# Denominators and Q masks by DMA, the quotient on GpSimd, V products in pairs, zero products as fillers, in a two-branch attention kernel

## The chip, the cores and the metric

The kernel runs on one core of a Trainium2 chip. A core has a matrix engine (PE, TensorE), a vector engine (DVE), a scalar engine (ACT) that computes exponentials, GpSimd (POOL), a sync engine (SP) that here only issues DMAs, and 16 DMA engines. Each engine works through its own instructions in order, and they wait for one another with semaphores. Matrix products are written to PSUM, which has 8 banks of 128 partitions by 512 fp32 numbers; everything else lies in SBUF.

The metric is the device time of one execution in microseconds (us), as the median of several.

## The reference

One input `x` of 2048 positions by 512 features goes through two attention blocks, each with 32 heads of 16 features. A sigmoid gate mixes the two results.

```python
g = sigmoid((x * gate_w).sum(-1, keepdims=True))
# A: linear attention, phi(q) = [softmax(q w), softmax(-q w)], the same for k
kv  = einsum("bhsf,bhsd->bhfd", phi_k, v)
num = einsum("bhqf,bhfd->bhqd", phi_q, kv)
den = einsum("bhqf,bhf->bhq", phi_q, phi_k.sum(s)) + 1e-6
a = (num / den) @ A_wo
# B: ordinary attention
p = softmax((q @ k.T) * 16 ** -0.5)
b = (p @ v) @ B_wo
return g * a + (1 - g) * b
```

B is the large part: 32 heads times 2048 queries times 2048 keys make 134 million exponentials.

## The kernel before

**Tiles.** B is cut into 32 blocks. A block has four heads and 512 queries (`b // 8` is the chunk of queries, `b % 8` the group of heads). For each head there are 16 key tiles of 128 keys, so a block has 64 score tiles of 128 keys by 512 queries, and the kernel has 2048. A score tile is one product with K = 32 rows (`qk_mm`): the four heads of a group use four row strips of the array and can run side by side. Q is kept in `qz` twice, once for the even and once for the odd heads, with the other 16 rows of every 32 at zero.

**Two ways to an exponential.** Most tiles go to ACT (`add_exp`, L776). The tiles of ACT are taken in *slots* of three and two by turns; each slot has its own PSUM banks (`psS` 0 to 2 and 3 to 4), one ACTIVATE makes the exponentials of a slot, and the scores of slot j + 2 can be written only when slot j is read. The rest, `DN[b]` tiles of block b (416 in all), is done by DVE in *groups* of four (`add_group`, L736): a tile is drained to int16 with an added constant (D1, L749, one for each tile, out of the PSUM banks `psM` or `psS` 5), then over a whole group come D2 (L759) and D3 (L761), which split it by bit masks, and D4 (L764, a product). For every third group from the eighth on, GpSimd does D4 in four quarters (L767). Each such tile then needs two products with V (its *terms*, s and t) instead of one. A group may hold tiles of two blocks.

**V products.** `add_pv` multiplies the exponentials of a slot with V (L792). V carries a column of ones, so that row 16 of every 32 output rows is the sum of the weights. The four heads use four column strips of the array and add into one bank, `psO`. The exponentials lie in a ring of ten slots. `add_pvd` adds the terms of DVE's tiles.

**End of a block** (`add_norm`, L861). DVE transposes `psO` to SBUF (T1, L864), which frees the bank for the next block. It then takes the reciprocal of the sums (L867), multiplies (L870, into `TB`), and after each second block transposes back (T2, L874) into `oT`, the left operand of the output products. Those (`out_tile`, L899) add A and B into one bank; DVE scales the sum (L903) and SP writes it out (L887).

**Q.** `q_fill` (L594) makes two groups of heads for 512 queries: four PE products, and two DVE operations (L601) that multiply by the masks for even and odd heads into `qz`.

**Branch A and the rest** fill in beside B: weights and projections (L534, L561), `phi` (L953: two ACT exponentials, L965 and L967 on DVE, a product on GpSimd, L969), `kv_half`, `q_rest`, and the gate (L922, 64 products of one column).

**The order** of every engine's instructions is written out in advance by a planner (`Plan.layout`, L130). It simulates the five engines with a cost for each operation. Of the operations that are ready it takes the one with the lowest priority number. A `dq` (the score product of a DVE tile) or a `term` can ride with a running product of the same kind if its strip is free. PE's busy share in the last 3.4 us of the plan steers the fillers: below `ACTIVE[0]` an idle PE gets a product into a free bank of `psM` or `psS` 5 (L1101), and below `ACTIVE[1]` or `ACTIVE[3]` a score product gets one or two fillers ahead of it, written to its own bank of `psS` (L704). `emit` (L284) then gives each engine its list with the waits. So a wait on the chip holds up all that stands behind it on that engine, also where the plan saw none.

Of the kernel before, what the change touches and what calls it, by code (L numbers as in the profile page):

```python
# [8 lines left out]
BF16 = mybir.dt.bfloat16  # L9
# [20 lines left out]
DN = (0, 8, 10, 13, 11, 9, 13, 11, 3, 11, 7, 11, 13, 15, 18, 6, 15, 14, 18, 10, 15, 17, 20, 12, 17, 15, 16, 20, 16, 18, 17, 17)  # L30
G_EARLY = 8
D_FIRST = 12
RIDE = 0.02
WINDOW = 3.4
ACTIVE = (0.64, 0.66, 0.60, 0.54)
PE_CLASS = {"qk": 0, "dq": 0, "pv": 1, "term": 1}
T_PRIO = -10.0
G_DEEP = 5
K_AT, K_PACE, Q_AT, Q_PACE = 70.0, 8.0, 199.0, 12.5
POOL_GROUPS = tuple(range(8, 110, 3))  # L40
D_AHEAD = 20.0
# [8 lines left out]
class Op:  # L50
    __slots__ = ("eng", "dur", "prio", "fn", "deps", "succ", "nd", "ready", "end", "lat", "sem", "count",
                 "name", "full", "extra", "room", "fill", "bank_of", "acq", "rel", "seq", "clock", "take", "pos", "margin", "done", "kind", "heads", "lock", "tight")

    def __init__(self, eng, dur, prio, fn, name):
        self.eng, self.dur, self.prio, self.fn, self.name = eng, dur, prio, fn, name
        self.deps, self.succ = [], []
        self.lat, self.sem = 0.0, None
# [5 lines left out]
        self.done = False  # L63
        self.kind, self.heads, self.lock = None, (), False
# [20 lines left out]
class Plan:  # L85
# [44 lines left out]
    def layout(self):  # L130
# [16 lines left out]
        last_pe, used_heads, last_cls = None, set(), None  # L147
        lock_end = {"dve": 0.0, "pool": 0.0}
        while left:
# [5 lines left out]
            while finish and finish[0][0] <= t + 1e-9:  # L155
                _, _, phase, op = heapq.heappop(finish)
                op.done = op.done or phase == 1
                for s in op.succ:
# [4 lines left out]
                    else:  # L163
# [3 lines left out]
                        if op.sem is not None:  # L167
                            gap += MARGIN
                    s.ready = max(s.ready, (op.end if phase else op.end - op.lat) + gap)
# [8 lines left out]
            for e in ENGINES:  # L178
# [6 lines left out]
                ride = None  # L185
                if e == "pe" and last_pe is not None and busy[e] > t - 1e-6:
                    want = {"qk": "dq", "pv": "term"}[last_pe]
                    for item in sorted(queues[e]):
                        o = item[2]
                        if o.kind == want and not used_heads & set(o.heads):  # L190
                            if o.acq is not None:
                                bs = [b for b in o.acq.banks if b.free and b.shared]
# [31 lines left out]
                if e == "pe":  # L224
                    while streams and streams[0][1] < t - WINDOW:
                        streams.popleft()
                    active = sum(y - max(x, t - WINDOW) for x, y in streams) / WINDOW
# [21 lines left out]
                if e == "pe" and ride is None:  # L249
                    last_pe, used_heads = (op.kind, set(op.heads)) if op.kind in ("qk", "pv") else (None, set())  # L250
                if e == "pe":
                    if op.room and t > 20.0 and active < ACTIVE[1]:
                        op.extra = min(op.room, 1 if active > ACTIVE[2] else 2)
                        op.full += 0.21 * op.extra
                        op.dur += 0.105 + 0.215 * op.extra
# [4 lines left out]
                    if ride is None:  # L260
                        streams.append((t + op.dur - op.full, t + op.dur))
# [874 lines left out]
```

The softmax here doesn't subtract the row's maximum and nothing guards it: scores larger than these inputs give would overflow.

## Time and profile before

| | us |
|---|---|
| median of 8 runs | 806.74 |
| lowest and highest run | 802.97, 808.21 |
| the profiled execution | 806.11 |
| its span, from the first to the last instruction | 804.2 |
| ACT busy in it | 777.6 |
| PE, DVE, POOL busy in it | 754.3, 692.4, 231.6 |

The groups of instructions that the change touches, from the list of groups by shape (count, busy us and mean ns of one):

| line | engine, operation | count | busy us | mean ns |
|---|---|---|---|---|
| L779 | ACT exponentials, three tiles | 326 | 508.7 | 1560 |
| L779 | ACT exponentials, two tiles | 327 | 372.2 | 1139 |
| L704 | PE fillers ahead of scores | 133 | 47.6 | 406 |
| L1101 | PE fillers in idle time (`psS`, `psM`) | 15, 13 | 5.4, 5.1 | 383, 417 |
| L864 | DVE T1, transpose of `psO` | 32 | 22.5 | 702 |
| L867 | DVE reciprocal, 128x16 | 32 | 7.6 | 237 |
| L870 | DVE multiply into `TB` | 32 | 14.7 | 459 |
| L874 | DVE T2 | 16 | 11.2 | 703 |
| L601 | DVE Q masks (from `psM`, from `psS`) | 18, 12 | 13.0, 8.8 | 723, 736 |

The mean of one instruction is longer than its share of the busy time where instructions of one engine overlap: the 653 exponentials of B together keep ACT busy for 749.8 us, 1.148 us each. Idle time of an engine is put down to the instruction that came after it, and to the one that released that.

### The profile page before, as it was taken

Reading aid. Unit: us, or ns where it says so; the run is one execution under the profiler, and the core shown is the slowest. Engines: PE = TensorE matmul, PEld = TensorE weight load, DVE = VectorE, ACT = ScalarE, POOL = GpSimd, SP = SyncE. Lnnn points to the kernel's source line nnn. Section 1 sums busy time; section 2 is a strip of 40 time slices with the busy share of each in tenths; the row PEclk is TensorE's granted clock in tenths of the full one; section 3 lists DMA queues with packets and bytes.
Section 4 is the critical chain, followed back from the end, with each engine's and each line's share of the span. In section 5 each row is a group of like instructions: output and inputs, shape, how many; then the busy total and the mean of one; then the engine's idle time right before and its main releaser. Section 6 shows DMA issues by size and latency. Waiting matters only on the chain.

```text
span 804.2 us, 14104 instructions
## 1 busy us (share of the span) xinstructions
PE 754.3 (94%) x5959; PEld 229.6 (29%) x5959; DVE 692.4 (86%) x1120; ACT 777.6 (97%) x724; POOL 231.6 (29%) x188
## 2 busy tenths in 40 slices
PE   8999999999999999999899989999989999998899
PEld 4333332333323232232232222322222222212223
DVE  3488878978766898898999999999999999989995
ACT  5999999999999999999999999999999999988996
POOL 5000022252443132522323333242222422342222
PEclk9899999999999999999999999999999999978999
DMA  5600000000100000000000000000000000000000
GB/s 126 138 2 1 1 2 1 1 1 1 54 0 2 1 7 14 1 9 1 1 1 2 2 1 1 1 14 2 15 1 1 7 1 14 8 0 1 1 1 27
DMA packets 18958, 9.30 MB, mean 12 GB/s; under 512 B 13264, under 2 KB 18896, under 8 KB 18896
## 3 DMA queue, kind: packets, MB, share of 16 engines
q1 hardware_dynamic: 17408, 7.74, 3.9%
q8 instruction: 46, 0.75, 0.4%
q10 hardware_dynamic: 1104, 0.66, 0.3%
q0 software_dynamic: 384, 0.02, 0.1%
q14 instruction: 16, 0.13, 0.1%
HBM read 3.69 MB, written 2.10 MB: 7 GB/s over the span
## 4 chain that ended last, share of the span: by engine, by line
ACT 70%; PE 21%; DVE 6%; SPq 1%; issue 1%; POOL 1%; DMA 0%
ACT E_t L779 67%; PE psS L687 6%; PE psO L792 6%; PE psS L534 3%; ACT EA_t L960 3%; PE psM L534 3%; PE psS L704 1%; SPq L431 1%; DVE Tx_t L749 1%; DVE vA_t L749 1%; DVE WB_t L759 1%; POOL WAT_t L767 1%; DVE vA_t L761 1%; PE psM L687 1%; DMA xT_t<-in_A_x_dram 0%
## 5 line engine op out<-in xcount | busy, mean ns | idle before, releaser
L779 ACT ACTIVATE E_t<-psS 128x1536 bf16<-128x1536 f32 (+1 forms) x653 | 749.8, 1349 | 13.0 <-PE psS L687 10.4
L687 PE MATMUL psS<-qz_t,kTB_t 32*128 32x512 bf16 x1831 | 277.9, 390 | 33.3 <-ACT E_t L779 26.6
L792 PE MATMUL psO<-E_t,vaug_t 128*32 128x512 bf16 (+1 forms) x1632 | 242.5, 395 | 0.0
L687 PEld LDWEIGHTS psS<-qz_t,kTB_t 32*128 32x128 bf16 x1831 | 68.2, 91 | 269.5 <-ACT E_t L779 200.7
L767 POOL TENSOR_TENSOR Tx_t<-Tx_t,WB_t 128x512 bf16<-128x512 bf16 x44 | 53.7, 1249 | 144.3 <-DVE WAT_t L761 43.9
L792 PEld LDWEIGHTS psO<-E_t,vaug_t 128*32 128x32 bf16 (+1 forms) x1632 | 56.5, 93 | 128.8 <-issue 124.9
L749 DVE TENSOR_SCALAR Tx_t<-psM 128x512 int16<-128x512 f32 x103 | 70.4, 684 | 22.4 <-PE psM L687 20.5
L767 POOL TENSOR_TENSOR vA_t<-vA_t,WB_t 128x512 bf16<-128x512 bf16 x44 | 53.2, 1239 | 122.7 <-DVE WB_t L759 51.2
L687 PE MATMUL psM<-qz_t,kTB_t 32*128 32x512 bf16 x217 | 84.7, 390 | 2.3 <-DVE Tx_t L749 0.6
L792 PE MATMUL psO<-vA_t,vaug_t 128*32 128x512 bf16 (+1 forms) x304 | 76.2, 389 | 0.0
L749 DVE TENSOR_SCALAR Tx_t<-psS 128x512 int16<-128x512 f32 x85 | 57.8, 681 | 7.1 <-PE psS L687 4.3
L749 DVE TENSOR_SCALAR vA_t<-psS 128x512 int16<-128x512 f32 x71 | 48.3, 680 | 6.5 <-PE psS L687 4.5
L704 PE MATMUL psS<-xT_t,ident_t 128*128 128x512 bf16 x133 | 47.6, 406 | 6.6 <-ACT E_t L779 6.0
L965 DVE TENSOR_REDUCE stat_t<-EA_t 128x64 f32<-128x1024 bf16 x32 | 38.8, 1213 | 16.6 <-ACT EA_t L960 16.3
L969 POOL TENSOR_TENSOR phiK_t<-EA_t,stat_t 128x1024 bf16<-128x1024 bf16 x16 | 33.2, 2079 | 65.0 <-DVE stat_t L967 65.0
L767 POOL TENSOR_TENSOR phiQ_t<-phiQ_t,WoA_t 128x512 bf16<-128x512 bf16 x16 | 18.0, 1154 | 116.5 <-DVE phiQT_t L761 116.5
L792 PE MATMUL psO<-Tx_t,vaug_t 128*32 128x512 bf16 (+1 forms) x188 | 51.4, 383 | 0.0
L767 POOL TENSOR_TENSOR WAT_t<-WAT_t,WB_t 128x512 bf16<-128x512 bf16 x24 | 29.8, 1271 | 64.0 <-DVE WB_t L759 21.5
L749 DVE TENSOR_SCALAR vA_t<-psM 128x512 int16<-128x512 f32 x65 | 44.4, 683 | 4.1 <-PE psM L687 2.9
L969 POOL TENSOR_TENSOR phiQ_t<-EA_t,stat_t 128x1024 bf16<-128x1024 bf16 x16 | 32.3, 2020 | 43.2 <-DVE stat_t L967 43.2
L792 PE MATMUL psO<-WAT_t,vaug_t 128*32 128x512 bf16 (+1 forms) x156 | 44.0, 401 | 0.0
L764 DVE TENSOR_TENSOR Tx_t<-Tx_t,WB_t 128x2048 bf16<-128x2048 bf16 x24 | 29.1, 1211 | 0.1
(177 smaller groups left out, 948.8 us busy)
## 6 DMA issues: line engine op xcount, KB each, us to landing
out_dram<-WvA_t SPq DMA_DIRECT2D x14, 128.0 KB, 1.7
WB_t<-in_B_wqkv_dram SPq DMA_DIRECT2D x3, 384.0 KB, 4.6
WvA_t<-in_A_wqkv_dram SPq DMA_DIRECT2D x1, 512.0 KB, 4.1
WoA_t<-in_A_wo_dram SPq DMA_DIRECT2D x1, 512.0 KB, 3.9
WoB_t<-in_B_wo_dram SPq DMA_DIRECT2D x1, 512.0 KB, 4.9
phiK_t<-in_A_x_dram SPq DMA_DIRECT2D x2, 128.0 KB, 2.8
phiK_t<-in_A_x_dram ACTq DMA_DIRECT2D x2, 128.0 KB, 3.0
WB_t<-in_B_wqkv_dram SPq DMA_DIRECT2D x2, 128.0 KB, 3.8
```

The costliest lines, as they stand in the source:

```text
L431: dma("sp", 0.01 * (4 * c + t), lambda e, c=c, t=t: e.dma_start_transpose(xT[:, t, NQ * c:NQ * (c + 1)], A_x[0, NQ * c:NQ * (c + 1), 128 * ...
L534: return [lambda e, ap, i=i: e.matmul(ap, lhsT=lhs[i], rhs=rhs[i], start=(i == 0), stop=(i == len(lhs) - 1)) for i in range(len(lhs))]
L687: return e.matmul(bank, lhsT=kT_B[32 * i:32 * i + 32, hg // 2, 128 * kt:128 * (kt + 1)], rhs=qz[32 * i:32 * i + 32, (b // 8) % 2, hg, :], ...
L704: e.matmul(psS[:, 512 * base:512 * (base + 1)], lhsT=ident[:], rhs=xT[:, 0, 0:NQ], start=True, stop=True)
L749: ops.append(drain(f, mm, "dve", 0.70, d_prio(d), lambda e, ap, q=q: e.tensor_scalar(quarter(t, q).bitcast(I16), ap, EXPB, 0.0, op0=ALU.ad ...
L764: add(1.24, lambda e: e.tensor_tensor(shaped(t, m), shaped(t, m), m, ALU.mult), [g["m"]], tk, "D4")
L767: ops.append(P.add("pool", 1.0, d_prio(g["ts"][0]) - 5.0, lambda e, q=q: e.tensor_tensor(quarter(t, q), quarter(t, q), quarter(m, q), ALU. ...
L779: op = P.add("act", 0.051 + 0.4267 * n, 0.0, lambda e: e.activation(Ebuf[:, j // 2 % EPAIRS, 1536 * (j % 2):1536 * (j % 2) + 512 * n], psS ...
L792: return e.matmul(psO[32 * i:32 * i + w, :], lhsT=vaug[:, kt, VW * h:VW * h + w], rhs=rhs, start=start, stop=stop, tile_position=(0, 32 * ...
L960: ins = e.activation(EA[:, b, :].rearrange("p (g s c) -> p s g c", s=2, c=64)[:, sgn, :, :], ap.rearrange("p (g c) -> p g c", c=64), ACTF. ...
L965: P.add("dve", 1.22, prio, lambda e: e.tensor_reduce(stat[:, b, 1, :], e3, AX.X, ALU.add), reads=[("EA", b)], writes=[("ss", b)], name=f"s ...
L969: P.add("pool", 2.0, prio, lambda e: e.tensor_tensor(dst.rearrange("p (g f) -> p g f", f=DH), e3, stat[:, b, 1, :].unsqueeze(2).to_broadca ...
```

## The change

- **Q masks.** `q_fill` keeps one DVE operation, a scaled copy of all rows for the even heads. Four DMAs on SP (`qo`) then copy the odd heads' rows to the other half of `qz`, and four more (`qe`) copy zeros over them in the first half. The zeros come from two memsets of `qz` on GpSimd in the beginning, planned at 3.3 and 4.3 us.
- **Weight sums and quotient.** For blocks 0 to 29, DVE copies `psO` as it is to `Tf` (L864's place). The sums go through DRAM: one DMA writes the four rows of sums (`ld`), one reads them back spread over 128 partitions by 16 (`lq`). After each second block four DMAs put the odd heads' rows beside the even ones (`mg`), DVE takes one reciprocal of 128x32, one DMA writes it to DRAM (`lr`), eight read it back, each to 16 partitions (`rb`), and GpSimd multiplies `Tf` by it into `oT`. All these DMAs are on SP. For odd groups of heads the V slice starts 16 columns earlier, so that the result lies in the upper 16 rows. Blocks 30 and 31 keep the old way.
- **Groups end with their block.** All `DN` are even (420 tiles in all), so a block's last group has two or four tiles. `PN` gives the number of groups of each block whose D4 is on GpSimd (33 in all). The buffers go by three phases (blocks 0 to 7, 8 to 13, 14 on) instead of two.
- **V products in pairs.** `hold` makes the V product of an even slot wait for the exponentials of the odd slot after it.
- **Fillers.** Those ahead of score products are gone. A V product with a head that has started gets up to two products of a zero weight tile of 32 columns, added into that head's strip of `psO`. The planner weighs PE's activity by the kind of product (`ROWS` for one to four score tiles side by side, 0.9 and 1.1 for terms and V products), with thresholds of 0.42 to 0.48, and counts riding products in part.
- **Planner and pace.** `dq` and `term` can ride behind one another as well, if they were ready when the stream began. Terms have priority 40 instead of -10. The gate is in four parts. Branch A's K side begins at slot 96 with pace 5 (before: 70 and 8), its Q side at 202 with pace 19 (199 and 12.5), and both are held back by the exponentials of given slots (Q side: slot 260 and every 20 from there).

```diff
-WINDOW = 3.4
-ACTIVE = (0.64, 0.66, 0.60, 0.54)
+WINDOW = 3.41
+ROWS = (0.0, 0.28, 0.58, 0.75, 0.8)
+ACTIVE = (0.46, 0.44, 0.48, 0.42)
-T_PRIO = -10.0
+T_PRIO = 40.0
+PV_SETS, PV_FROM = 2, 0
+DMA_PAD, T2_PAD = 1.0, 1.5
...
+    pool(3.3, -7, lambda e: e.memset(qz[:, 0, 2:8, :], 0.0), writes=["qza"], name="qz0")
+    pool(4.3, -7, lambda e: e.memset(qz[:, 1, :, :], 0.0), reads=["qza"], writes=["qz0"], name="qz1")
...
+    def moves(kind, fn, n, reads, writes, name, lat=2.0):
...
+        op = P.add("sp", 0.07 * n, -40, fn, reads=reads, writes=writes, name=name, sem=chain[kind][0], lat=lat)
+        op.semval = chain[kind][1]
+        op.pad = DMA_PAD
+        return op
...
     def q_fill(r, qc, prio, banks=None, after=()):
...
-        for par in range(2):
...
+        drain(f, mm, "dve", 0.69, prio, lambda e, ap: e.tensor_single_scalar(qz[:, c, 2 * r, :], ap, QSCALE, ALU.mult),
+              writes=[("q", c, 2 * r)], name=f"Qe{r}.{qc}")
+        moves(f"qo{c}{r}", lambda e: [e.dma_start(qz[o, c, 2 * r + 1, :], qz[o, c, 2 * r, :]) for o in z(1)], 4,
+              [("q", c, 2 * r), "qz0"], [("q", c, 2 * r + 1)], f"qo{r}.{qc}")
+        moves(f"qe{c}{r}", lambda e: [e.dma_start(qz[o, c, 2 * r, :], qz[y, c, 2 * r + 1, :])
+                                      for o, y in zip(z(1), z(0))], 4,
+              [("q", c, 2 * r + 1)], [("q", c, 2 * r)], f"qe{r}.{qc}")
...
-            for _ in range(op.extra):
-                e.matmul(psS[:, 512 * base:512 * (base + 1)], lhsT=ident[:], rhs=xT[:, 0, 0:NQ], start=True, stop=True)
...
+    def hold(j):
+        k = j + (PV_SETS - 1 - (j + PV_FROM) % PV_SETS)
+        return [exp_ops[k]] if k > j and k < NS and exp_ops[k] is not None else []
...
+                for _ in range(zero_ops[j, b].extra):
+                    e.matmul(psO[32 * old[0]:32 * old[0] + 32, :], lhsT=zero[:], rhs=xT[:, 0, 0:NQ], start=False, stop=False,
+                             tile_position=(0, 32 * old[0]), skip_group_check=True)
...
     def add_norm(b, pv):
...
+        if b < NB - 2:
+            P.add("dve", 0.69, -50, lambda e: e.tensor_copy(Tf[:, par, :], psO[:]), reads=["psO"], writes=[("Tf", par)],
+                  after=[pv], name=f"ev.{b}")
+            moves(f"ld{par}", lambda e: e.dma_start(ld[par], Tf[16 - par::32, par, :]), 1, [("Tf", par)], [("ld", par)],
+                  f"ld{b}")
+            moves(f"lq{par}", lambda e: e.dma_start(Lq[:, par, :], ld[par].rearrange("i (a c) -> (i a) c", c=16)), 1,
+                  [("ld", par)], [("Lq", par)], f"lq{b}")
+            if par == 1:
+                moves("mg", lambda e: [e.dma_start(Tf[32 * i + 16:32 * i + 32, 0, :], Tf[32 * i + 16:32 * i + 32, 1, :])
+                                       for i in range(4)], 4, [("Tf", 1)], [("Tf", 0)], f"mg{b}")
+                P.add("dve", 0.35, -40, lambda e: e.reciprocal(rd[:], Lq[:]), reads=[("Lq", 0), ("Lq", 1)],
+                      writes=["rd2"], name=f"rd{b}")
+                moves("lr", lambda e: e.dma_start(lr.rearrange("t i (a c) -> (i a) t c", c=16), rd[:]), 1, ["rd2"],
+                      ["lr"], f"lr{b}")
+                moves("rb", lambda e: [e.dma_start(Rb[32 * i + 16 * t:32 * i + 16 * t + 16, :],
+                                                   lr[t, i].unsqueeze(0).to_broadcast([16, D]))
+                                       for i in range(4) for t in range(2)], 8, ["lr"], ["Rb"], f"rb{b}")
+                P.add("pool", 1.1, -40, lambda e: e.tensor_tensor(oT[:, qc % 2, r, :], Tf[:, 0, :], Rb[:], ALU.mult),
+                      reads=[("Tf", 0), "Rb"], writes=[("oT", qc % 2, r)], name=f"T2.{b}").lock = True
+                P.ops[-1].pad = T2_PAD
```

## The prediction

> **What bounds the kernel now.** First the page's busy shares and its slices, then ACT in order of time, then busy time by stage.
>
> ```profile
> PE 754.3 (94%) x5959; PEld 229.6 (29%) x5959; DVE 692.4 (86%) x1120; ACT 777.6 (97%) x724; POOL 231.6 (29%) x188
> ...
> ACT  5999999999999999999999999999999999988996
> ...
> PEclk9899999999999999999999999999999999978999
> ```
>
> ACT works without a break from 20 us to the end, but for the slices where the granted clock of PE dips. ACT's idle time is 804.2 - 777.6 = 26.6 us; 13.0 of it lie before exponentials of B, and 2.7 of these in the first 24 us (2.06, 0.50, 0.16). The rest of B's waits, in ACT's timeline, are 15 gaps of 9.3 us together. The larger ones:
>
> ```profile
> 37.42 1.02 ACT L779 ACTIVATE E_t<-psS 128x1024 bf16<-128x1024 f32 x1 [0.88 <-PE psS L687]
> ...
> 390.70 36.27 ACT L779 ACTIVATE E_t<-psS 128x1024 bf16<-128x1024 f32 x32 [1.37 <-PE psS L687]
> ...
> 605.38 100.75 ACT L779 ACTIVATE E_t<-psS 128x1024 bf16<-128x1024 f32 x89 [0.81 <-PE psM L687]
> ...
> 716.90 18.45 ACT L779 ACTIVATE E_t<-psS 128x1536 bf16<-128x1536 f32 x16 [1.03 <-PE psS L687]
> ```
>
> Now the stretches around these times (columns: us, then busy us and instructions of PE, PEld, DVE, ACT, POOL, then the granted clock):
>
> ```profile
> 383.10:386.50 3.40, 2.30 (x15) 0.67 (x13) 3.27 (x7) 3.40 (x5) 2.14 (x2) 1.00 0.00 0
> 386.50:389.90 3.40, 3.40 (x24) 0.96 (x22) 2.99 (x5) 2.83 (x4) 0.59 (x1) 0.50 0.00 0
> 598.10:601.50 3.40, 2.36 (x14) 0.59 (x12) 3.40 (x7) 3.40 (x4) 0.00 (x0) 1.00 0.00 0
> 601.50:605.00 3.50, 3.50 (x26) 0.55 (x23) 3.09 (x5) 3.00 (x3) 0.00 (x0) 0.51 0.00 0
> 703.90:707.40 3.50, 2.23 (x13) 0.57 (x10) 3.36 (x6) 2.96 (x3) 3.50 (x4) 0.99 0.00 0
> 707.40:717.60 10.20, 10.20 (x40) 1.59 (x39) 7.98 (x13) 7.40 (x7) 0.59 (x1) 0.50 0.00 0
> ...
> 660.00:700.00 40.00, 37.71 (x297) 10.28 (x293) 39.51 (x58) 40.00 (x36) 10.96 (x8) 1.00 0.03 11
> ```
>
> The clock is halved in five stretches: 31.5 to 38.3, 386.5 to 389.9, 601.5 to 605.0, 707.4 to 717.6 and 734.7 to 741.5, 30.7 us in all. Of the 9.3 us of late gaps 8.6 lie in or right behind them, 0.28 us of stall for each us at half clock; the others are 0.54 and 0.17. Just ahead of each halving PE did little: 13 to 15 products in 3.4 us, where the 40 us from 660 have 297, or 25 in 3.4. So the end is set by ACT's work, plus what PE's clock costs it, plus start and tail.
>
> Why PE was thin is seen in the timeline from 702 us on:
>
> ```profile
> 702.69 5.31 POOL L767 TENSOR_TENSOR vA_t<-vA_t,WB_t 128x512 bf16<-128x512 bf16 x4 [10.09 <-DVE WB_t L759]
> ...
> 703.13 1.64 DVE L761 TENSOR_SCALAR vA_t<-Tx_t 128x2048 int16<-128x2048 int16 x1
> ...
> 705.42 0.39 PE L687 MATMUL psS<-qz_t,kTB_t 32*128 32x512 bf16 x1 [1.06 <-DVE Tx_t L749]
> ```
>
> PE waits 1.06 us for DVE to drain a bank, and DVE is late since one mask took 1.64 us beside GpSimd instead of the usual 0.68. At 598 and 731 PE waits for ACT at the end of a block, with V products scarce.
>
> **ACT's work.** 2048 - 420 = 1628 tiles make 651 slots instead of 653, two of two tiles fewer. With 749.8 us for 326 + 327 exponentials and 1560 - 1139 = 421 ns between the forms, one of two tiles costs (749.8 - 326 x 0.421) / 653 = 0.94 us: **-1.9 us**, certain.
>
> **The clock.** From the records I summed PE's stream time (0.213 us for 512 columns, products on different strips once) over the windows of 3.41 us in which the clock changes, with the new planner's weights (0.28, 0.58, 0.75, 0.8 for one to four score tiles side by side, 1.1 for V products and full ones). Of 226 windows at full clock, the end aside, the five just ahead of a halving are the five lowest: 0.22, 0.28, 0.32, 0.32, 0.35; the next is 0.38. So these weights order the windows as the gate does, and it lies at about 0.37. The new thresholds, 0.42 to 0.48, are above it, where the old ones (0.64 and so on) were met in the plan and missed on the chip: both filler banks are the ones DVE was late to free, and the fillers at L704 stand ahead of scores that ACT awaits. A zero product needs no bank, since it adds into `psO`, and delays no score ahead of it. Bounds: all 9.3 us go, or none and more (third rival). I take a third of the 8.6 left over, since the planner's times still differ from the chip's, most around a block's first V product, where no filler may start: **-6.5 us** with the 0.54 and 0.17 partly gone.
>
> What the Trainium skill would have here speaks against a gain ("TensorE: Matmul & The Clock Gate", section "Why this matters for your kernels"): it asks for no PE-idle gap above some 3 us, and no such gap precedes any of the five halvings, so by it the fillers would be worth nothing and the time 804.8. The rows above decide otherwise: products were spaced 1 us apart and the clock fell all the same.
>
> **DVE.** Off: 15 masks x 0.73 = 11.0; 30 reciprocals x 0.237 = 7.1; 30 multiplies x 0.459 = 13.8; 15 T2 x 0.703 = 10.5. On: 15 reciprocals of 128x32, between the rows for 16 and 64 columns (0.237, 0.542), 0.35 taken, 5.1; four tiles' D1, 2.7; 12 half groups instead of five whole ones, about 3 (half-size rows are not shown; bounds 0.34 and 0.69 for D2 and D3); gate 0.5. T1 becomes a copy of the same size (drains of 128x512 take 0.68, T1 0.70). Sum -31 us of 692. DVE is not on the path but in the late stretches (39.5 of 40 us busy from 660), and there it gains little: Q tiles of A, 4.6 us of DVE each by their rows, are now paced up to slot 560 and more, where before the last ran at 528 us, and `PN` gives GpSimd 6 groups of the last eight blocks instead of 11. So I count **0** from it, -0.7 to +2 as bounds.
>
> **GpSimd.** 15 quotients at the 1.15 to 1.27 us of L767 add 18 us, a group more 5, and the memsets, 7168 columns at L486's 0.545 us for 512, 7.6. The memsets stand ahead of `gw` and `Wbd`, which end at 12.2 us and so at 20; their readers come at 40 slots or later. **0.** Queued behind a quotient that waits for `rb` are D4 quarters and `phi` products, and behind these terms on PE. POOL is idle 71% of the time; without that cover a wait of w us delays terms by w.
>
> The Trainium skill states that GpSimd and DVE share a port pair which one of them holds for a whole instruction ("SBUF — State Buffer", section "SBUF: two separate sides"). The 1.64 us mask above agrees. By the rule each of the 15 quotients may hold DVE for its length, 15 x 1.2 = 18 us of DVE; by the row, 15 x (1.64 - 0.68) = 14 us; in both the planner's locks and DVE's free 14% cover it.
>
> **SP.** 15 x 8 for masks, 30 x 2, and 15 x (4 + 1 + 8) are 375 DMAs. An issue takes 0.33 us (output) to 0.45 (x), so SP is busy 124 to 169 us, and the plan's 0.07 is too low. What waits in this queue holds up the others: `qe` for `qo`, `lq` for `ld`, `rb` for `lr`, and outputs behind all. Landing takes 1.7 (output) to 3.0 us (x), planned 2.0 with pads of 1.0 and 0.6, which absorb the issue but for `rb` (8 x 0.38 = 3.0 against 0.56). Q is filled seven blocks ahead. **0**, as long as the quotient's chain fits: `Tf` is free for the next even block only after the quotient. Low end: copy 0.70, three landings of 1.7, reciprocal 0.24, `rb` 7 x 0.33 + 1.7, quotient 1.15: 11 us. High end: 0.71, three of 3.0, 0.54, DVE's queue 1.2, `rb` 7 x 0.45 + 3.0, `mg` 1.8, a Q move 8 x 0.45 + 3.0, a D4 quartet 5.3, 1.27: 33 us. I take 17 (landings of 2.2, issues of 0.38, half a quartet). An even block has at least 48 ACT tiles x 0.459 = 22 us.
>
> **Pairs.** A V product starts one exponential later, up to 1.4 us, and so may a block's copy. The ring of ten slots (11.5 us) covers it; the last slot, 650, is flushed alone, so the tail stays. A change between scores and V products on PE is saved every second slot, worth nothing while PE waits for ACT 200.7 us. **0**, -0.5 to +2.
>
> **Sum.** 804.2 - 1.9 - 6.5 = 795.8 us of span. The profiled execution has 1.9 us outside its span and lies 0.6 below the median: **798.3 us**. Its own range is 795.5 (9.3 + 1.9 off the median) to 801.
>
> **Rivals.**
> 1. *DVE stays the late engine.* For it: 39.5 of 40 us, and PE's 1.06 us wait. A filler cannot pass a blocked PE. Then the three halvings from 600 us on stay and only those at 31 and 386 (1.5 + 1.4 us) go: 806.74 - 1.9 - 2.9 = 802.
> 2. *The quotient's chain outlasts a block.* From 22 us on, the copy of `psO` waits for `Tf`, PE stops at the next block's first V product, the scores behind it are late and ACT stalls. For it: 375 issues on one queue, the in-order waits, the high end of 33. Against it: 17 by the nearest rows. At 4 us in 6 of 15 pairs: +24, 822.
> 3. *The zero products don't hold the clock.* No row shows one. Some 25 windows lie between 0.38 and 0.50; if their fillers fail, each costs 3.4 x 0.28 = 0.95 us: 806.74 - 1.9 + 24 = 829.
> 4. *Gain and new waits cancel*, the fillers finding no place: 806 to 808.
>
> **Chances.** Forecast 0.56, first rival 0.19, second 0.11, third 0.08, fourth 0.06. A difference under 0.2% (1.6 us) can't be told from none here. So faster 0.75, same 0.06, slower 0.19. The range, 794.5 to 812, takes in the first and the fourth rival and the mild forms of the second.
>
> **What would show it.** Granted clock 1.00 in nearly all stages and ACT's gaps after 24 us under 4 us in all: the clock step is right. 651 exponentials at 1.148 us: ACT's work. First rival: half clock after 600 us, behind waits for D1. Second: DVE's copy of `psO` waiting for GpSimd or a DMA, with ACT gaps at block ends. Third: more half clock than 30.7 us. I am wrong if the clock holds and ACT still idles, or if start or tail, which I leave as they are (2.7 us of gaps, 8.6 us from the last exponential's end at 795.6), change by over 2 us.

## The result and the profile after

The changed kernel takes **817.19 us** (median of 20 executions, 810.2 to 826.67), the kernel before on the same chip 807.56. The ratio is **1.0107**, 95% interval 1.0089 to 1.0125: slower, where faster was forecast. (The ratios here leave out executions over 1.5% above their kernel's fastest, so one can be smaller than that of the medians.) The profiled execution took 817.24 us, its span 815.4 against 804.2. From the page of the changed kernel: busy time by engine, the slices of ACT and of PE's granted clock, and three groups (count, busy us and mean ns of one, idle time before them):

```profile
PE 737.6 (90%) x5929; PEld 229.7 (28%) x5929; DVE 675.3 (83%) x1076; ACT 776.3 (95%) x722; POOL 245.3 (30%) x198
...
ACT  5999999999998999999999999999999999998996
...
PEclk9998999999998899899999999999999999997999
...
L821 ACT ACTIVATE E_t<-psS 128x1536 bf16<-128x1536 f32 (+1 forms) x651 | 747.2, 1324 | 25.9 <-PE psS L728 22.2
...
L883 PE MATMUL psO<-xT_t,zero_t 128*32 128x512 bf16 x100 | 34.0, 431 | 0.0
...
L918 DVE COPY Tf_t<-psO 128x512 f32<-128x512 f32 x30 | 20.5, 683 | 12.6 <-PE psO L835 12.6
```

The exponentials' line of the kernel before:

```profile
L779 ACT ACTIVATE E_t<-psS 128x1536 bf16<-128x1536 f32 (+1 forms) x653 | 749.8, 1349 | 13.0 <-PE psS L687 10.4
```

ACT's own work shrank as counted: 747.2 / 651 = 1.148 us for an exponential, as before. What grew is the idle time ahead of the exponentials, 13.0 us before and 25.9 now, 25.4 of it behind scores. The granted clock dips in more slices. In ACT's timeline the larger gaps look like this (start, length, then the idle time ahead in brackets):

```profile
304.24 6.28 ACT L821 ACTIVATE E_t<-psS 128x1536 bf16<-128x1536 f32 x5 [0.58 <-PE psS L728]
...
403.21 9.22 ACT L821 ACTIVATE E_t<-psS 128x1536 bf16<-128x1536 f32 x8 [0.83 <-PE psS L728]
...
742.53 4.84 ACT L821 ACTIVATE E_t<-psS 128x1536 bf16<-128x1536 f32 x4 [1.24 <-PE psS L728]
748.71 6.88 ACT L821 ACTIVATE E_t<-psS 128x1536 bf16<-128x1536 f32 x6 [1.34 <-PE psM L728]
```

Busy time by stretch around two of them, and the stretch from 660 us on that was shown of before (us; busy us and instructions of PE, PEld, DVE, ACT, POOL; clock; DMA share; GB/s):

```profile
298.40:301.80 3.40, 2.35 (x21) 0.61 (x19) 3.40 (x5) 3.40 (x4) 0.07 (x1) 1.00 0.00 0
301.80:305.20 3.40, 3.40 (x15) 0.76 (x13) 2.86 (x6) 2.82 (x3) 0.00 (x0) 0.50 0.00 0
...
735.30:738.70 3.40, 2.84 (x23) 0.84 (x20) 3.40 (x6) 3.40 (x4) 1.27 (x1) 1.00 0.13 28
738.70:749.00 10.30, 9.48 (x48) 1.95 (x48) 7.30 (x13) 7.72 (x8) 6.66 (x6) 0.50 0.02 3
660.00:700.00 40.00, 34.76 (x279) 10.59 (x276) 38.46 (x63) 37.15 (x34) 8.55 (x7) 0.93 0.05 12
```

As before, PE does little in one stretch while ACT is fully busy, and in the next the clock is 0.50 and ACT falls behind. But there are now 15 such stretches after 24 us in place of 5, with 71.9 us in all in place of 30.7 (counted in stretches that begin after 24 us, to the end of the clock's records).

**How late ACT is, and when.** Short lateness hides in "busy": the record of an exponential runs some 0.2 us past the start of the next (for three tiles 1533 ns long, with the next 1331 ns after its start), so lateness below that leaves no gap. So I took the time from the start of each exponential to that of the one right behind it. Its median is 1.331 us after three tiles and 0.904 after two in both kernels; what goes beyond, by more than 0.025 us, is lateness. It is put down to half clock where the next exponential starts in a halved stretch, up to 0.5 us ahead of it or up to 1 us behind it. Summed after 24 us:

| kernel | us at half clock | late at half clock | late at full clock | span |
|---|---|---|---|---|
| before | 30.7 | 11.1 | 9.9 | 804.2 |
| changed | 71.9 | 20.3 | 13.4 | 815.4 |

The span's +11.2 us is +9.2 at half clock, +3.5 at full clock, -1.9 of ACT's work, -0.6 in the tail and some +0.9 in the first 24 us. The ten added stretches cost 0.92 us each.

The same relation holds from execution to execution. Half-clock time is twice the missing clock times the length. Over the executions of the changed kernel (granted clock 0.940 to 0.973) a line through time against half-clock time has a slope of 0.33 us per us and meets zero at 794.8 us; for the kernel before, over 89 executions beside the experiments, 0.32 and 796.5. These end points are extrapolated, the first with an error of 1.3 us, so that a gain of some 2 us at an equal, full clock is likely but not shown.

**Why PE is thin.** PE's timeline from 299 us on, ahead of the halving at 301.8:

```profile
299.19 0.39 PE L728 MATMUL psS<-qz_t,kTB_t 32*128 32x512 bf16 x2 [0.53 <-ACT E_t L821]
299.51 0.60 PE L835 MATMUL psO<-E_t,vaug_t 128*32 128x512 bf16 x5
...
301.45 0.39 PE L728 MATMUL psS<-qz_t,kTB_t 32*128 32x512 bf16 x2 [0.53 <-ACT E_t L821]
301.77 0.60 PE L883 MATMUL psO<-xT_t,zero_t 128*32 128x512 bf16 x1
```

One pair of V products stands between the waits for ACT, with no zero product; the next pair, 2.27 us later, brings one, too late. In the plan this pair also has none. A zero product can come only with V products, thus once in two slots, an idle filler only where a bank stands free, and the stretch that the clock's records show is 3.4 us long. In the 3.4 us ahead of the 15 halvings PE ran 7 to 13 score products, 3 to 9 of V and terms, and no zero product (eight times), one (four) or two (three); all of these ten start in the last 0.3 us. In the whole execution there are 127 fillers (100 zero products, 27 idle fills) in place of 161, and V products and terms run four side by side 471 times in place of 331, so that the same work keeps PE busy for less time. By the weights of the prediction 23 windows of 3.41 us lie below 0.42; before there were 10.

The planner's own measure can be taken at the same places of PE's order. Ahead of nine of the 15 halvings it was 0.34 to 0.40, below every threshold: the plan itself is thin there. Ahead of the other six it was 0.43 to 0.49, and PE was thinner on the chip than planned.

In two stretches of the 15 PE's longest wait is for DVE. The first is the one at 260.9. GpSimd's timeline in the changed kernel has a product of the linear branch:

```profile
255.41 2.25 POOL L1046 TENSOR_TENSOR phiK_t<-EA_t,stat_t 128x1024 bf16<-128x1024 bf16 x1 [7.84 <-DVE stat_t L1044]
```

DVE's timeline has a mask that starts beside it:

```profile
255.79 2.42 DVE L804 TENSOR_SCALAR WAT_t<-Tx_t 128x2048 int16<-128x2048 int16 x1
```

And PE's has the score that waits behind it:

```profile
258.86 0.38 PE L728 MATMUL psS<-qz_t,kTB_t 32*128 32x512 bf16 x1 [1.60 <-DVE Tx_t L787]
```

A mask of usually 0.7 us takes 2.42 beside the GpSimd product and ends 0.55 us after it, the drain of the bank stands behind the mask, and PE waits 1.60 us. This is the longest idle time of PE between 24 and 795 us. The second is the one at 499.8, with the second longest, 1.24 us: PE's timeline puts it down to ACT, but the weight load of the same score waits for a drain that stands behind a mask of 1.64 us:

```profile
496.35 1.64 DVE L804 TENSOR_SCALAR vA_t<-vA_t 128x2048 int16<-128x2048 int16 x1
...
498.64 0.09 PEld L728 LDWEIGHTS psM<-qz_t,kTB_t 32*128 32x128 bf16 x1 [1.73 <-DVE Tx_t L787]
```

Ahead of six more halvings (69.7, 400.8, 527.1, 632.9, 660.2 and 738.7) at least half of PE's waits over 0.15 us are for DVE, 0.21 to 0.65 us in all; ahead of the other seven all are for ACT.

### The profile page after: what moved, and what is told of

It reads as the page before. It is cut to its first block, busy times and chain, and to the rows that moved or that the text cites. A ratio compares the mean times of both kernels' runs of the same rounds, so it can differ in the third digit from the quotient of the medians.

```text
span 815.4 us, 14529 instructions
## 1 busy us (share of the span) xinstructions
PE 737.6 (90%) x5929; PEld 229.7 (28%) x5929; DVE 675.3 (83%) x1076; ACT 776.3 (95%) x722; POOL 245.3 (30%) x198
## 4 chain that ended last, share of the span: by engine, by line
ACT 68%; PE 17%; DVE 11%; issue 2%; SPq 1%; DMA 1%
ACT E_t L821 65%; PE psS L728 5%; PE psO L835 5%; ACT EA_t L1037 3%; DVE Tx_t L787 2%; PE psS L556 2%; PE psM L556 2%; DVE WB_t L802 2%; PE psO L883 1%; SPq L450 1%; DVE WAT_t L804 1%; DVE Tx_t L807 1%; DVE vA_t L787 1%; DVE vA_t L804 1%; PE psM L728 1%
## 5 line engine op out<-in xcount | busy, mean ns | idle before, releaser
L821 ACT ACTIVATE E_t<-psS 128x1536 bf16<-128x1536 f32 (+1 forms) x651 | 747.2, 1324 | 25.9 <-PE psS L728 22.2
L728 PE MATMUL psS<-qz_t,kTB_t 32*128 32x512 bf16 x1839 | 298.6, 398 | 58.3 <-ACT E_t L821 44.6
L835 PE MATMUL psO<-E_t,vaug_t 128*32 128x512 bf16 x1628 | 236.0, 405 | 0.0
L787 DVE TENSOR_SCALAR Tx_t<-psS 128x512 int16<-128x512 f32 x121 | 82.6, 683 | 29.8 <-PE psS L728 20.7
L934 POOL TENSOR_TENSOR oT_t<-Tf_t,Rb_t 128x512 bf16<-128x512 f32 x15 | 19.3, 1287 | 203.8 <-DMA Rb_t<-lr 203.8
L835 PEld LDWEIGHTS psO<-E_t,vaug_t 128*32 128x32 bf16 x1628 | 51.6, 95 | 96.4 <-issue 84.5
L835 PE MATMUL psO<-vA_t,vaug_t 128*32 128x512 bf16 (+1 forms) x272 | 46.5, 392 | 0.8 <-DVE vA_t L804 0.8
L807 DVE TENSOR_TENSOR Tx_t<-Tx_t,WB_t 128x2048 bf16<-128x2048 bf16 (+1 forms) x39 | 45.6, 1169 | 0.2
L835 PE MATMUL psO<-Tx_t,vaug_t 128*32 128x512 bf16 x236 | 43.5, 392 | 0.0
L802 DVE TENSOR_SCALAR WB_t<-Tx_t 128x2048 int16<-128x2048 int16 (+1 forms) x48 | 33.4, 695 | 1.7 <-POOL Tx_t L810 1.6
L883 PE MATMUL psO<-xT_t,zero_t 128*32 128x512 bf16 x100 | 34.0, 431 | 0.0
L918 DVE COPY Tf_t<-psO 128x512 f32<-128x512 f32 x30 | 20.5, 683 | 12.6 <-PE psO L835 12.6
```

The lines of the kernel that those rows point to most:

```text
L728: return e.matmul(bank, lhsT=kT_B[32 * i:32 * i + 32, hg // 2, 128 * kt:128 * (kt + 1)], rhs=qz[32 * i:32 * i + 32, (b // 8) % 2, hg, :], ...
L787: ops.append(drain(f, mm, "dve", 0.70, d_prio(d), lambda e, ap, q=q: e.tensor_scalar(quarter(tb, q).bitcast(I16), ap, EXPB, 0.0, op0=ALU.a ...
L802: add(0.72 if full else 0.45, lambda e: e.tensor_scalar(shaped(mi, mi), shaped(ti16, mi), 0x007F, 0x3F00, op0=ALU.bitwise_and, op1=ALU.bit ...
L807: add(1.24 if full else 0.72, lambda e: e.tensor_tensor(shaped(t, m), shaped(t, m), m, ALU.mult), [g["m"]], tk, "D4")
L821: op = P.add("act", 0.051 + 0.4267 * n, 0.0, lambda e: e.activation(Ebuf[:, j // 2 % EPAIRS, 1536 * (j % 2):1536 * (j % 2) + 512 * n], psS ...
L835: return e.matmul(psO[32 * i:32 * i + w, :], lhsT=vaug[:, kt, o:o + w], rhs=rhs, start=start, stop=stop, tile_position=(0, 32 * i), skip_g ...
```

## The experiments

In the tables "half" is the time at half clock after 24 us, "late" ACT's lateness at half and at full clock, both of the profiled execution. "All" is the half-clock time of the whole span, as twice the missing clock times the span, on average over the executions of a kernel; for the kernel before it is 34 us, for the changed one 72.

**1. The quotient's chain.** `a3_no_chain` drops its DMAs after the first two blocks:

```diff
+    gone = {o for o in P.order["sp"] if o.name[:2] in ("ld", "lq", "mg", "lr", "rb") and int(o.name[2:]) > 1}
+    ...
+        P.order[e] = [o for o in P.order[e] if o not in gone]
```

> The changed kernel, same order, but after the first two blocks the sums' DMAs (to DRAM, back, the merge of odd heads, the reciprocals to DRAM and back: 240 of 375 DMAs) are left out; the quotient takes the first pair's values, so the output is wrong. Clock theory: 813 to 819 with 60 to 75 us at half clock, as in the changed kernel. Rival of the transfers: under 808, with the gaps of ACT at the ends of blocks gone.

Measured 817.54 us, ratio 1.014 (1.011 to 1.0171), half 62.2 (all: 69), late 22.8 and 9.7. So 238 of 375 DMAs (17 of the chain's 255 stay) and their waits are worth nothing that shows. The waits of the changed kernel say the same (total us, count, longest):

```profile
POOL oT_t L934 <- DMA Rb_t<-lr: 203.8, 12, 61.0
...
DVE Tf_t L918 <- PE psO L835: 12.6, 5, 8.3
```

GpSimd stood idle for 203.8 us until `Rb` landed, and this costs nothing: DVE's copy waits for PE alone, never for the quotient. The 120 DMAs of the masks have no run of their own; no wait of PE over 0.15 us is for them.

**2. Do zero products hold the clock, and what do they cost?** The planned order is kept; only their number changes. `a2_no_zero` sets all to 0; `a1_zero_each_pair` gives every pair at least one; `b1_before_zero` puts one into every second V product of the kernel before; `e1_zero_full` makes 96 of the 100 as wide as the array.

```diff
+    for op in zero_ops.values():                      # a2_no_zero
+        op.extra = 0
+    for (j, b), op in zero_ops.items():               # a1_zero_each_pair
+        if j >= 20 and j % 2 == 0 and op.room:
+            op.extra = max(op.extra, 1)
-    zero = sb([128, 32], name="zero")                 # e1_zero_full
+    zero = sb([128, 128], name="zero")
...
+                        e.matmul(psO[:], lhsT=zero[:], rhs=xT[:, 0, 0:NQ], start=False, stop=False, skip_group_check=True)
```

> The changed kernel, same order, without any of its 100 zero products. Clock theory: they hold the clock in part, so half clock rises over 90 us and the time over 822. If zero products don't count for the gate: half clock 60 to 75 us, and 812 to 818, the same or a little better since PE has less to do. Rival of the transfers: 812 to 818.

> The changed kernel with every engine's order as it is, but one zero product at least with the first V product of every pair from slot 20 on (some 300 in place of 100). Clock theory (the changed kernel is slower since PE is too thin between its pairs and the clock is halved for 68 us instead of 31): under 15 us at half clock, ACT gaps after 24 us under 9 us (22.5 in the changed kernel), 797 to 804. Rival (the new transfers and the quotient on GpSimd make PE wait): the waits stay and PE has more to do, 812 or more. Rival (a zero product of 32 columns doesn't count for the clock gate): half clock stays at 60 us or more.

> The kernel before, same order, with one zero product of 32 columns ahead of the V products of every second slot from slot 20 on (some 300, each 0.21 us of PE), its other fillers kept. Clock theory: under 10 us at half clock instead of 31, ACT gaps after 24 us under 4 us instead of 9.3, 797 to 802. If zero products don't count for the gate: half clock 25 us or more and 806 or more. If PE's time is what is short: ACT waits at full clock, 810 or more.

> The changed kernel, same order, 96 of its 100 zero products as full 128x128 products over the whole output bank instead of one strip of 32 columns. If the gate counts columns, so that a strip weighs a quarter: half clock falls from 72 us to under 40 and the time to 803 to 810. If it counts rows or streams alone, as the new weights say: 60 to 85 us at half clock and 813 to 821.

| kernel | zero products | us | ratio | half | all | late |
|---|---|---|---|---|---|---|
| `a2_no_zero` | 0 | 846.12 | 1.0461 (1.0419 to 1.0503) | 215.5 | 205 | 52.5, 9.4 |
| changed | 100 | 817.19 | 1.0107 (1.0089 to 1.0125) | 71.9 | 72 | 20.3, 13.4 |
| `a1_zero_each_pair` | 358 | 821.96 | 1.0177 (1.0138 to 1.0215) | 20.7 | 25 | 8.7, 27.3 |
| `b1_before_zero` | 293 | 820.0 | 1.0162 (1.0131 to 1.0193) | 24.1 | 22 | 9.4, 26.1 |
| `e1_zero_full` | 100 | 825.14 | 1.0228 (1.0194 to 1.0261) | 64.9 | 82 | 18.4, 15.0 |

(The profiled execution of `a2_no_zero` was its slowest, 853.98 us; that of `e1_zero_full` its fastest, 818.14.)

Page lines of `a2_no_zero`, the clock and the exponentials:

```profile
PEclk9699999999997787669999876999698797786899
...
L821 ACT ACTIVATE E_t<-psS 128x1536 bf16<-128x1536 f32 (+1 forms) x651 | 752.3, 1308 | 52.3 <-PE psS L728 44.8
```

The same of `a1_zero_each_pair`, with its zero products:

```profile
PEclk9999999999999997999999999999899999999999
...
L821 ACT ACTIVATE E_t<-psS 128x1536 bf16<-128x1536 f32 (+1 forms) x651 | 750.3, 1289 | 24.4 <-PE psS L728 16.9
...
L883 PE MATMUL psO<-xT_t,zero_t 128*32 128x512 bf16 x358 | 130.4, 391 | 0.4 <-issue 0.3
```

Zero products hold the clock: between the profiled executions the 100 save 215.5 - 71.9 = 143.6 us at half clock and 52.5 - 20.3 = 32 us of lateness, and on average over all executions 205 - 72 = 133 us at half clock. But they aren't free. With 258 more the clock is nearly whole and the time no better, since scores now come late at full clock: (27.3 - 13.4) / 258 = 0.054 us for each. The kernel before gives the same price: (26.1 - 9.9) / 293 = 0.055. The shown idle time before the exponentials hides it (24.4 against 25.9); the busy time does not (750.3 against 747.2). My expectation of `a1_zero_each_pair` and `b1_before_zero` left this out and missed. The full-width products don't raise the clock (all: 82 against 72, the medians 8 us apart the wrong way), so a 32-column product serves the clock no worse than a full one.

**3. Zero products where PE would idle.** The order is kept again; a pass after the planning puts zero products into gaps of the planned PE order, where no score has to wait for them. `c1_gap_zero` takes gaps over 0.3 us, `c2_gap_more` over 0.2 (two above 0.45), `c3_gap_only` these without the 100 ahead of V products; `b2_before_gap` does the first in the kernel before.

```diff
     P.layout()
+    ...
+    for op in P.order["pe"]:
+        gap = op.end - op.lat - op.dur - ends
+        if strip is not None and gap > 0.3 and ends > 20.0:
+            ...
+                row.append(z)
+        row.append(op)
+        ends = op.end - op.lat
```

> The changed kernel, same order, its 100 zero products kept, plus 152 more that stand in the plan's idle gaps of PE (over 0.3 us) inside a block, behind the product that ends before the gap, so that they delay no score in the plan. The theory now: a halved clock costs 0.28 us a us, a zero product ahead of V products costs some 0.06 us as it makes scores late, and one in a gap costs little. Expected: under 25 us at half clock (72 in the changed kernel), late scores at full clock 13 to 18 us (13.4), 800 to 807. If PE's load as such is what costs: like a1, 815 to 822.

> The kernel before, same order, its fillers kept, plus 44 zero products in the plan's idle gaps of PE. Theory: half clock down from 31 to under 20 us, 800 to 806. If the thin windows of this kernel come from waits that the plan does not see, the gaps of the plan are the wrong places: 805 to 810.

> The changed kernel in its order, with 249 zero products in the gaps of its planned TensorE order over 0.2 us (152 over 0.3 us in the run before). Theory (half-clock time is what the change lost, and zero products in gaps hold no score up): less than 15 us at half clock, exponentials late by 11 to 15 us at full clock, 798 to 806 us. Rival (every zero product costs 0.05 us of a late score, wherever it stands): 97 more cost 5 us, 808 to 813 us.

> The same 249 zero products in gaps, and the changed kernel's own 100 ahead of V products left out. Theory (gaps are enough for the clock, and a zero product ahead of a V product costs 0.04 to 0.05 us of late score): less than 25 us at half clock and 4 us less late at full clock than with them, 795 to 804 us. Rival (the planner's thin windows have no gap to fill, so its own 100 are needed): over 50 us at half clock, above 808 us.

| kernel | in gaps | us | ratio | half | all | late |
|---|---|---|---|---|---|---|
| `c1_gap_zero` | 152 | 805.56 | 0.9976 (0.9952 to 1.0001) | 13.7 | 25 | 6.1, 11.5 |
| `c2_gap_more` | 249 | 809.69 | 1.0036 (1.0013 to 1.006) | 17.1 | 25 | 9.9, 14.3 |
| `c3_gap_only` | 249, none ahead of V | 808.19 | 1.001 (0.9983 to 1.0037) | 27.6 | 32 | 10.1, 12.2 |
| `b2_before_gap` | 44 | 806.58 | 0.9972 (0.9953 to 0.999) | 34.1 | 29 | 11.8, 10.5 |

The page of `c1_gap_zero`:

```profile
PEclk9999999999999799999999999999999999999999
...
L821 ACT ACTIVATE E_t<-psS 128x1536 bf16<-128x1536 f32 (+1 forms) x651 | 745.4, 1354 | 11.4 <-PE psS L728 9.6
```

Its PE timeline, with the same products as at 299.19 in the changed kernel:

```profile
298.38 0.39 PE L728 MATMUL psS<-qz_t,kTB_t 32*128 32x512 bf16 x2
298.70 0.61 PE L835 MATMUL psO<-E_t,vaug_t 128*32 128x512 bf16 x5
...
300.05 0.60 PE L1200 MATMUL psO<-xT_t,zero_t 128*32 128x512 bf16 x2
300.64 0.39 PE L728 MATMUL psS<-qz_t,kTB_t 32*128 32x512 bf16 x2
```

Two zero products fill the 0.53 us that PE had waited for ACT, the scores behind them start as soon after the V products as before (1.94 us both times), and the clock holds. Half-clock time falls from 71.9 to 13.7 us and full-clock lateness does not rise (11.5 for 13.4): the change's loss is its clock, as the theory says, and undoing it takes back 817.2 - 805.6 = 11.6 us. The profiled execution was the run's fastest (801.04; 810.8 the slowest, clock 0.977); over all executions half-clock time falls from 72 to 25 us. Two stretches remain in it, and the longer, 10.2 us from 258.8 on, has the same 1.60 us wait for DVE ahead of it: that wait is not in the plan. In `c2_gap_more`, smaller gaps bring no more clock and part of the cost returns, 14.3 - 11.5 = 2.8 us for 97: the rival's 808 to 813 was met. Without the 100 ahead of V products 27.6 us of half clock remain, and `c3_gap_only` misses its 795 to 804. In the kernel before, 44 in gaps give about 0.3%. In the profiled execution its half-clock time did not fall, but over its 12 executions it is 29 us, against 35 over the 23 of the kernel before that ran with them: by the slope of 0.32 us per us these 6 us are worth 1.9, most of the 2.3 us gained.

**4. Which part thins PE?** Each kernel here is planned anew with one part changed: `r1_after_nopair` without pairs (`PV_SETS = 1`), `act50` with thresholds 0.04 higher, `f1_old_fillers` with the fillers, measure and thresholds of before, `n1_one_rider` with the old limit on packing, `t1_term_prio` with the old priority of terms, and `p1_before_pairs`, the kernel before with pairs.

```diff
-PV_SETS, PV_FROM = 2, 0                       # r1_after_nopair
+PV_SETS, PV_FROM = 1, 0
-ACTIVE = (0.46, 0.44, 0.48, 0.42)             # act50
+ACTIVE = (0.50, 0.48, 0.52, 0.42)
-T_PRIO = 40.0                                 # t1_term_prio
+T_PRIO = -10.0
-                    want = {"qk": "dq", "dq": "dq", "pv": "term", "term": "term"}[last_pe]   # n1_one_rider
+                    want = {"qk": "dq", "pv": "term"}.get(last_pe)
```

> The changed kernel planned anew without pairs (each V product waits for its own slot alone); the plan itself is 7.6 us longer and has 76 zero products instead of 100. If pairs make PE thin: under 45 us at half clock, and 810 or less in spite of the longer plan. If not: 60 us or more and 818 to 828.

> The changed kernel planned again with its thresholds 0.04 higher (0.50, 0.48 and 0.52 for 0.46, 0.44 and 0.48); the plan then holds 132 zero products for 100. Theory (a filler can come only with a V product, so higher thresholds don't reach the windows that have none): 40 to 65 us at half clock, 809 to 816 us. Rival (the thresholds alone were too near the point at which the clock drops): under 30 us at half clock, 798 to 805 us.

> The changed kernel planned again with the fillers, the unweighted measure and the thresholds of the kernel before (full-array products ahead of scores, no zero products); everything else of the change is kept. The plan is 27 us longer than the changed kernel's. If the old fillers hold the clock where the zero products don't, under 45 us at half clock, but the scores that they stand ahead of come late: 820 to 840 us. If the denser packing of V products and terms thins TensorE whatever the fillers are, over 60 us at half clock and 830 to 845 us. If the change lost by its fillers alone and the plan's length is not met on the chip: 798 to 808 us.

> The changed kernel planned again with the old limit on packing: a mask product or a linear term may ride beside one score group or one V product, not beside another that rides already. The plan is 20 us longer than the changed kernel's (801.3 for 781.2), and both kernels so far ran some 20 to 34 us over their plans. Theory (the denser packing leaves TensorE thin in time): under 45 us at half clock, so 20 to 25 us over its plan, 823 to 828 us. Rival (packing is not what thins it): over 65 us at half clock and 830 to 840 us.

> The changed kernel planned again with the old priority of the linear terms' products (-10 for 40), so that they come as soon as they are ready instead of last. The plan is 786.0 us for 781.2. Theory (kept for last, they bunch up and leave thin windows between): under 45 us at half clock, 804 to 812 us. Rival (their place makes no difference to the clock): 60 to 90 us at half clock, 816 to 828 us.

> The kernel before with one part of the change, V products given out in pairs, planned again; its fillers, measure and thresholds are the old ones. The plan is 807.5 us for 784.8. Theory (V products that come only every second slot thin TensorE in between): over 60 us at half clock and 835 to 850 us. Rival (pairs are harmless to the clock): 25 to 45 us at half clock, 820 to 832 us, some 20 us over the plan as the kernel before is.

| kernel | plan, us | us | ratio | half | all | late |
|---|---|---|---|---|---|---|
| `r1_after_nopair` | 788.8 | 835.78 | 1.0337 (1.0291 to 1.0383) | 112.6 | 109 | 34.0, 16.4 |
| `act50` | 781.9 | 813.51 | 1.0079 (1.0048 to 1.011) | 47.8 | 45 | 16.6, 12.0 |
| `f1_old_fillers` | 808.6 | 843.87 | 1.0419 (1.0361 to 1.0477) | 71.7 | 67 | 24.0, 29.2 |
| `n1_one_rider` | 801.3 | 850.96 | 1.0521 (1.0452 to 1.059) | 105.8 | 97 | 52.1, 12.9 |
| `t1_term_prio` | 786.0 | 824.03 | 1.0102 (1.0041 to 1.0163) | 99.0 | 84 | 33.2, 8.3 |
| `p1_before_pairs` | 807.5 | 833.83 | 1.0326 (1.0258 to 1.0394) | 58.0 | 64 | 23.8, 22.0 |

(The profiled execution of `t1_term_prio` was its slowest, 829.08 us.) Higher thresholds bring half-clock time from 72 to 45 us and reach only part of the windows, as expected; in the time (1.0079 for 1.0107) the two intervals overlap. Every other part, undone alone, leaves 67 us or more at half clock on average, and neither `n1_one_rider` (theory and rival both under 840) nor `r1_after_nopair` came where it was expected. `p1_before_pairs`, between its two expectations, shows a cost of its own in its list of waits (total us, count, longest):

```profile
ACT E_t L779 <- PE psO L792: 23.5, 7, 8.5
```

ACT waits 23.5 us, 8.5 at most, for V products to free a slot of the ring of exponentials; that wait does not appear in the changed kernel, whose priorities and pacing were set with pairs. `n1_one_rider` has one such wait, of 16.3 us. So single parts can't be lifted out of a plan that was fitted as a whole, and these runs name no one culprit. All they agree on is that none of the older pieces would have held the clock in the new plan.

**5. Filling by the plan's own measure.** `c4_gap_thin` and `c5_gap_thin_more` fill gaps over 0.2 us only where the planned activity is below 0.54 and 0.62:

```diff
+        thin = sum(w * (y - max(x, begins - WINDOW)) for x, y, w in run) / WINDOW < 0.54
+        if strip is not None and begins - ends > 0.2 and ends > 20.0 and thin:
```

> The changed kernel in its order, with a zero product in a planned TensorE gap over 0.2 us only where the planned activity of the last 3.41 us is below 0.54: 104 of them for 152 by length of gap alone. Theory (what matters is that no window is thin; zero products elsewhere only make scores late): under 25 us at half clock, 10 to 12 us late at full clock, 796 to 803 us. Rival (the chip's thin windows are not the plan's, so that only fillers spread everywhere hold the clock): over 40 us at half clock, 808 to 815 us.

> The same with a bound of 0.62, which places 146 zero products, as many as by length of gap alone (152, 805.6 us) but in thinner places. Theory as for 104: under 20 us at half clock, 797 to 804 us. Rival: the place makes no difference, 804 to 807 us.

Measured 807.9 us, ratio 1.0012 (0.9984 to 1.0041), half 28.0 (all: 28), late 12.9 and 11.1; and 810.64 us, 1.0025 (0.9996 to 1.0055), half 34.1 (all: 31), late 16.6 and 11.9. Both keep the clock clearly better than the changed kernel and neither reaches its expected time. The plan's thin places are the chip's only in part. Of the versions run none is clearly faster than the kernel before; the best, `b2_before_gap` and `c1_gap_zero`, are 0.3% and 0.2% below it, at the edge of what was measured.

## Why the prediction was wrong

**The step that failed is the clock, -6.5 us; it measured +9.2.** Its argument was that the new thresholds, 0.42 to 0.48, lie above the gate at about 0.37, and that a zero product "needs no bank" and "delays no score ahead of it". The order of windows by weight held roughly: in the changed kernel the windows ahead of a halving lie at 0.27 to 0.42 (one at the very start aside), but the lowest that did not halve at 0.37, so the two overlap and the weights give no sharp gate. (The count of 13 to 15 products ahead of each halving was misread for two of the five: 37 and 16 ran ahead of those at 31.5 and 734.7. The weights, not the count, put these among the lowest.) What failed is the step from a threshold to a window. The threshold of the zero products is asked only when V products are issued, once in 2.27 us at the thin places, and a zero product can't be put between. So a plan that hugs its threshold leaves windows under the gate: 23 below 0.42 where the kernel before had 10, nine of the 15 that halved planned so, six thinner on the chip than in the plan. I had named the place where no filler may start (a block's first V product) and sized it as a third of the old loss, instead of asking how often a filler can start at all.

**Rival 3 had the right price under the wrong condition.** It said that zero products don't hold the clock, and that each failed window costs 0.95 us. They do hold it (`a2_no_zero`); the ten added stretches cost 0.92 us each. Of its 25 windows 10 came.

**"Delays no score" failed too,** with a smaller size: a zero product ahead of V products costs 0.054 us of later scores where PE has no idle time, and close to nothing in a gap. With 100 of them this is up to 5 us, of which the +3.5 at full clock may be a part.

**What held.** ACT's work: -1.9 counted, 747.2 us for 651 measured against 749.8 for 653, -2.6. GpSimd and SP at 0: DVE's copy waits for PE alone, and without the chain the time is the same; rival 2 is refuted. Tail: -0.6, start: +0.9, both within the 2 us allowed. DVE at 0 held in part: rival 1, DVE late, explains two stretches of the 15, at 260.9 and 499.8, 13.7 of the 71.9 us at half clock, and may have a part in the six more where at least half of PE's waits are for DVE. The price of half clock, 0.28 us per us from visible gaps, is 0.36 before (11.1 / 30.7) and 0.28 changed (20.3 / 71.9) by the fuller count. Pairs at 0 are not settled: alone in the kernel before they cost 26 us, but in an order not fitted to them.

At full clock throughout the changed kernel would end near 795 us by the extrapolated line, below the 798.3 forecast. That was not reached: `c1_gap_zero` came to 805.6, with 25 us at half clock left on average over its executions.

## What to carry to other kernels

An activity filler is only as good as the places where it can be issued: compare the time between two such places with the length of the window over which the clock is decided, and put fillers into the waits of the queue rather than ahead of useful work, where each costs its share even if the profile shows no gap. A plan that fits a threshold closely has no reserve for what the chip does differently. When ACT is the bound, sum the distance between its starts, since lateness under the 0.2 us by which its records overlap here never appears as idle time.

## What the runs showed of the hardware

- A product with 32 columns counts for the clock no less than one with 128: 96 full-width zero products gave 82 us at half clock on average against 72, and a longer time. Products of nothing but zeros count as well (205 us without the 100).
- PE's clock was halved 15 times though PE never idled for longer than 1.60 us. The Trainium skill ("TensorE: Matmul & The Clock Gate", section "Why this matters for your kernels") asks, against drops in mid-kernel, for no PE-idle gaps above some 3 us; by the measurement that alone is not enough.
- The same order of instructions ran from 810.2 to 826.67 us with clocks of 0.973 to 0.940. The same page, in "Part 1: The HAM clock gate (the "warmup" mystery)", states that the window runs freely, so that where it falls on a program changes from run to run. That agrees with this spread; no run here varies the phase by itself.
- A mask on DVE took 2.42 us beside a GpSimd product of 2.25 us, in place of 0.7.
